# Raw weight blocks loaded ahead of the third and fourth attention chunk, and the first products moved accordingly

## The chip, the core and the metric

The kernel runs on one core of one Trainium2 chip. The metric is device time in microseconds of one execution. A profiled execution also gives a span, from its first to its last instruction.

## What is computed

Linear attention with decay over blocks of 64 positions, for 4 batches, 8 heads, 768 positions and a head size of 64; its output, as 3072 tokens of 512, goes through a two-layer network whose activation is h - tanh(h):

```
intra = einsum('bhic,bhjc->bhij', qb, kb) * Dmask[None]
intra = einsum('bhij,bhjd->bhid', intra, vb)
inter = einsum('bhid,bhde->bhie', qb * lam_pow[None], kv_state)
out[:, :, sl] = intra + inter
kv_state = lam_block * kv_state + einsum('bhsd,bhse->bhde', kb * rev_pow[None], vb)
...
h = x @ w_in            # 3072 x 512 by 512 x 2048
g = h - np.tanh(h)
return g @ w_out        # 2048 x 512
```

q, k, v are float32. The weights arrive as 64-bit floats, and the kernel reads them as pairs of 32-bit words.

## The kernel before

The sequence is cut into 6 groups of 128 positions; a group is taken for all 4 batches at once (512 tokens). One batch of a group is called a chunk here: chunks 0 to 3 are batches 0 to 3 of group 0. The change lies in group 0, the first some 40 us of the program.

**Loads.** All loads of this stage are issued by SP in the order of the program. `load(n)` issues q, k and v of chunks up to n (256 KB each, in pieces of 256 bytes). `load_weights(n)` issues raw blocks of `w_in` up to n: a block is 128 rows by 2 x 256 columns of 64-bit words, 512 KB. Blocks 0 and 1 of each unit come in one piece, blocks 2 and 3 in two halves of 64 rows. There are 16 blocks of `w_in`: block 4u + i holds rows i of unit u, and unit u is 512 of the 2048 hidden features. Four buffers hold raw blocks, so block n + 4 is loaded once block n is rounded as far as it reads the raw data.

**Rounding.** `round_block` makes a float32 block from a raw one. ScalarE makes two passes over it, called r (the low words, scaled, `AF.Copy`) and Abs (the high words, `AF.Abs`, into the block itself). VectorE then makes four passes: a clamp (L265), shift and mask (L267), the merge with the high word (L269) and the addition of r (L271). `weights(n)` rounds blocks up to n. For units 0 and 1 (`first`) the two ScalarE passes and the clamp are tied to the order of the program; the scheduler places the others.

**Attention.** For a chunk, `att_transpose` transposes q and k on TensorE (tp) and ScalarE copies them out (qt, kt); `att_decay` scales k by the decay on VectorE; `att_scores` forms the scores (sp), which VectorE multiplies by the mask (ss). For two chunks, `att_state` forms the state (kv), copied out by ScalarE, and `att_out` the output (op), which ScalarE copies to xt, the input of the first layer.

**First layer.** Group 0 goes through plain products. `up_plain(u, cs)` forms unit u for two of four quarters of its output, named 11, 21, 12 and 22: the second digit says which pair of chunks, the first which half of the unit's features. It is a generator: with `yield` between its steps the program puts other work between them. Each (i, c) is two products (h, 256 columns) by block i, so quarter 11 of unit u needs blocks 4u to 4u + 3 in turn. Then ScalarE forms the Tanh (th) and VectorE the difference (g).

In group 0 the work of TensorE, the copies of ScalarE and the masks of VectorE are tied: each engine has them in the order in which the program writes them. The second layer and the other five groups, which use two levels of Strassen-like products with weights from intermediate buffers in memory, are untouched.

Of the kernel before, what the change touches and what calls it, by code (L numbers as in the profile page):

```python
# [13 lines left out]
AF = mybir.ActivationFunctionType  # L14
# [9 lines left out]
def kernel(  # L24
# [32 lines left out]
    nc = tc.nc  # L57
    B, H, S, D = q.shape
# [3 lines left out]
    KI = DM // 128  # L62
# [55 lines left out]
    def tied(yes, op):  # L118
        return tc.keep_in_program_order(op) if yes else op
# [25 lines left out]
    def load(n):  # L145

        while at["loaded"] < min(n, len(chunks)):
            g, b = chunks[at["loaded"]]  # L150
            if g < GB:
                raw[g, b] = {}
                load_natural(g, b, "qkv")
                at["loaded"] += 1
                continue
            for b in range(B):
                raw[g, b] = {}
            nat = "kv" if g < NG - 1 else "v"

            first = (0, 1, 2) if g == GB else ()  # L160
            for b in first:
                load_natural(g, b, nat)
            for b in range(B - 1):
                load_blocks(g, b, "qk")
            load_blocks(g, 3, "q")
            for b in (0, 1):
                if b not in first:
                    load_natural(g, b, nat)
            load_blocks(g, 3, "k")
            for b in (2, 3):  # L170
                if b not in first:
                    load_natural(g, b, nat)
            at["loaded"] += B
# [31 lines left out]
    def load_weights(n):  # L205

        while ready["loaded"] < min(n, len(blocks)):
            if moe_w_in.dtype != F32:
                raw64 = stage.tile([128, 2, 256], I64, name="raw64", tag="raw64", bufs=WAHEAD)
                block = blocks[ready["loaded"]]  # L210
                load_block(nc.sync if block[0] == "in" else nc.gpsimd, raw64, *block, block[0] == "in")
                wraw[ready["loaded"]] = raw64
            ready["loaded"] += 1
# [38 lines left out]
    def round_block(w, raw64, first):  # L252


        word = raw64.rearrange("p a n -> p (a n)").bitcast(U32).rearrange("p (n w) -> p n w", w=2)
        wordf = raw64.rearrange("p a n -> p (a n)").bitcast(F32).rearrange("p (n w) -> p n w", w=2)
        lo, hi = word[:, :, 0], word[:, :, 1]
        w = w.rearrange("p a n -> p (a n)")
        wb, wi = w.bitcast(U32), w.bitcast(I32)

        r = stage.tile([128, 512], I32, name="r", tag="r", bufs=2)
        tied(first, nc.scalar.activation(r, lo, AF.Copy, scale=2.0 ** -29))  # L262

        tied(first, nc.scalar.activation(w, wordf[:, :, 1], AF.Abs))
        tied(first, nc.vector.tensor_scalar(out=w, in0=w, scalar1=CLAMP, scalar2=None, op0=AL.max))  # L265

        nc.vector.tensor_scalar(out=wb, in0=wb, scalar1=3, scalar2=0x3FFFFFF8, op0=AL.logical_shift_left,  # L267
                                op1=AL.bitwise_and)
        nc.vector.scalar_tensor_tensor(out=wb, in0=hi, scalar=0xC0000000, in1=wb, op0=AL.bitwise_and,  # L269
                                       op1=AL.bitwise_or)  # L270
        nc.vector.tensor_tensor(wi, wi, r, op=AL.add)  # L271

    def bank(name, tag, bufs):
        return psum.tile([128, 512], F32, name=name, tag=tag, bufs=bufs)


    load(B - 1)
    load_weights(2)
    load(B)
    load_weights(WAHEAD)  # L280

# [11 lines left out]
    def att_transpose(g, bs):  # L293
        for b in bs:
            load(g * B + b + 1)
            t = raw[g, b]
            qt = work.tile([128, NP, BLK], F32, name="qt", tag="qt")
            kt = work.tile([128, NP, BLK], F32, name="kt", tag="kt")
            for dst, x in ((qt, "q"), (kt, "k")):
                if g >= GB:  # L300
                    tc.keep_in_program_order(nc.vector.transpose(out=dst.rearrange("d p i -> d (p i)"),
                                                                 in_=t[x + "b"].rearrange("d p r a -> d (p r a)")))
                else:
                    tp = bank("tp", "att", 4).rearrange("d (p s) -> d p s", p=NP)
                    for p in range(NP):
                        tied(g == 0 or p == 0, nc.tensor.transpose(out=tp[:, p, :], in_=t[x][:, 2 * p:2 * p + 2, :],
                                                                   identity=ident))
                    tied(g == 0, nc.scalar.activation(dst, tp, AF.Copy))
            qd = None
            if g > 0:  # L310
                qd = work.tile([128, NP, BLK], F32, name="qd", tag="qd")
                nc.vector.tensor_tensor(qd, qt, fwd, op=AL.mult)
            tr[g, b] = (qt, kt, qd)

    def att_scores(g, bs):
        for b in bs:
            qt, kt, _ = tr[g, b]

            sp = [bank("sp", "att", 4).rearrange("s (p i) -> s p i", p=NP) for _ in range(2)]
            for p in range(NP):  # L320
                for j in range(2):
                    tied(g == 0, nc.tensor.matmul(out=sp[j][:, p, :], lhsT=kt[ts(j, 64), p, :],  # L322
                                                  rhs=qt[ts(j, 64), p, :], start=True, stop=True))
            ss = work.tile([128, 2, NP, BLK], F32, name="ss", tag="ss")
            for j in range(2):
                tied(g == 0, nc.vector.tensor_tensor(ss[:, j], sp[j], mask[:, j], op=AL.mult))  # L326
            sc[g, b] = ss

    def att_decay(g, b):
        kp = raw[g, b]["k"].rearrange("s (p j) d -> s p j d", j=2)  # L330
        tied(g != 1, nc.vector.tensor_tensor(kp, kp, bwd, op=AL.mult))

    def att_state(g, bs):
        if g == NG - 1:
            return

        kv = bank("kv", "att", 4).rearrange("d (b p e) -> d b p e", b=2, p=NP)
        for n, b in enumerate(bs):
            kd, vn = raw[g, b]["k"], raw[g, b]["v"]
            if g > 0:  # L340
                att_decay(g, b)
            for p in range(NP):
                for j in range(2):
                    tied(g == 0, nc.tensor.matmul(out=kv[ts(j, 64), n, p, :], lhsT=kd[:, 2 * p + j, :],  # L344
                                                  rhs=vn[:, 2 * p + j, :], start=n == 0 and p == 0, stop=True,
                                                  skip_group_check=True))
        st = state[:, bs[0]:bs[0] + 2]
        if g > 0:
            nc.vector.tensor_tensor(st, st, lam_blk, op=AL.mult)
            nc.vector.tensor_tensor(st, st, kv, op=AL.add)  # L350
        else:
            tied(True, nc.scalar.activation(st, kv, AF.Copy))
# [382 lines left out]
    def up_plain(u, cs):  # L735

        hm = {}
        for c in cs:
            a, t = divmod(c - 11, 10)
            hm[c] = bank("h", ("ya", "yb", "z", "w")[2 * t + a], 1).rearrange("q (m c) -> q m c", m=2)  # L740
        for i in range(KI):
            for c in cs:
                a, t = divmod(c - 11, 10)
                for m in range(2):
                    tied(u == 0, nc.tensor.matmul(  # L745
                        out=hm[c][:, m, :], lhsT=w1[u][:, i, a, ts(m, 128)], rhs=xt[0, t][:, i, :],
                        start=m == 0 and i == 0, stop=i == KI - 1, skip_group_check=True))
            if i + 1 < KI:
                yield
        for c in cs:  # L750
            th = work.tile([128, 2, HB], F32, name="th", tag="th")
            nc.scalar.activation(th, hm[c], AF.Tanh)
            nc.vector.tensor_tensor(hidden(0, c)[:, u], hm[c], th, op=AL.subtract)
        yield
# [24 lines left out]
    for b in (0, 1):  # L779
        att_transpose(0, (b,))  # L780
        att_decay(0, b)
        att_scores(0, (b,))
    att_state(0, (0, 1))
    att_transpose(0, (2,))
    att_decay(0, 2)
    weights(1)
    att_out(0, (0, 1))
    att_scores(0, (2,))
    half = up_plain(0, (11, 21))
    next(half)  # L790
    weights(2)
    att_transpose(0, (3,))
    att_decay(0, 3)
    att_scores(0, (3,))
    next(half)
    weights(KI)
    att_state(0, (2, 3))
    att_out(0, (2, 3))
    next(half)
    weights(KI + 2)  # L800
# [124 lines left out]
```

## Time and profile before

| | |
|---|---|
| time, median of 4 runs | 674.13 us (673.76 to 674.88) |
| the profiled execution's own time | 673.76 us |
| its span | 672.0 us |
| TensorE busy | 662.3 us (99%) |
| VectorE busy | 481.1 us (72%) |
| ScalarE busy | 194.8 us (29%) |
| GpSimd busy | 199.9 us (30%) |
| HBM read and written | 103.55 MB, 24.38 MB |

In the profile, PE is TensorE's products, PEld its weight loads, DVE is VectorE, ACT is ScalarE, POOL is GpSimd, and SP issues loads. A float32 product shows as two records. A row of the timeline has the start, the duration, the engine, the line, the operation and its tiles, and in brackets how long the engine had been idle and what ended that. A row of the waits has the waiting engine, what it wanted, who released it, the total, the number and the longest. "Landing" is the time from a load's issue to its last byte's arrival. In a row of windows each engine has its busy microseconds and, in brackets, its instructions.

### The profile page before, as it was taken

What the parts mean: (1) busy time and instruction counts of PE and PEld (TensorE: products, weight loads), DVE (VectorE), ACT (ScalarE), POOL (GpSimd) and SP (SyncE); (2) the same over time, 40 slices, a digit from 0 to 9 for tenths busy, and PEclk for the clock granted to TensorE, in tenths of its full rate; (3) what the DMA queues carried; (4) which work ended last, traced back from release to release, by engine and by line L of the source; (5) the groups of instructions that cost most, each with busy time, mean ns of one, the idle gap of its engine ahead of it and who ended that gap; (6) DMA issues with size and microseconds to landing.
All of it is one profiled execution on the core that took longest, in us unless ns stands there. A gap on an engine that the chain in (4) does not pass through costs nothing.

```text
span 672.0 us, 12866 instructions
## 1 busy us (share of the span) xinstructions
PE 662.3 (99%) x4824; PEld 577.4 (86%) x4824; DVE 481.1 (72%) x872; ACT 194.8 (29%) x373; POOL 199.9 (30%) x345
## 2 busy tenths in 40 slices
PE   8899999999999999999999999999999999999998
PEld 7688855558888999988999988899988899988897
DVE  4797857894887872399896378888358978357753
ACT  3664432423331111333112343112333112334110
POOL 0001424217332334144345200255300244400251
PEclk9899999999999999999999999999999999999999
DMA  9869788969955977487898741698840676610395
GB/s 207 218 192 246 250 250 253 309 145 258 259 142 131 242 202 211 112 256 216 224 297 248 199 85 43 152 288 236 254 81 4 156 247 199 227 49 1 109 299 171
DMA packets 162717, 128.80 MB, mean 192 GB/s; under 512 B 133856, under 2 KB 135008, under 8 KB 162656
## 3 DMA queue, kind: packets, MB, share of 16 engines
q0 software_dynamic: 28976, 96.49, 45.2%
q1 hardware_dynamic: 133536, 31.50, 23.6%
q8 instruction: 38, 0.62, 0.4%
q14 instruction: 23, 0.19, 0.1%
q10 hardware_dynamic: 144, 0.00, 0.0%
HBM read 103.55 MB, written 24.38 MB: 190 GB/s over the span
## 4 chain that ended last, share of the span: by engine, by line
PE 97%; DMA 2%; SPq 1%; DVE 0%; ACT 0%; issue 0%; ACTq 0%
PE y L428 17%; PE y L690 11%; PE z L428 10%; PE zw L690 8%; PE h L745 8%; PE op L766 8%; PE w L637 5%; PE y L637 5%; PE y L512 4%; PE plain L637 3%; PE sp L322 3%; PE op L376 3%; PE z L512 2%; PE op L370 2%; PE kv L344 1%; PE w L512 1%
## 5 line engine op out<-in xcount | busy, mean ns | idle before, releaser
L602 POOL DMA_DIRECT2D wb<-fine x147 | 79.2, 539 | 113.7 <-PE y L690 48.6
L436 ACT ACTIVATE th<-g 128x512 f32<-128x512 f32 x76 | 47.6, 630 | 98.9 <-DVE g L441 33.2
L605 POOL DMA_DIRECT2D wb<-factors x56 | 30.2, 541 | 153.7 <-PE y L637 97.3
L428 PE MATMUL y<-xt,w 128*128 128x256 f32 x320 | 74.0, 380 | 0.0
L428 PEld LDWEIGHTS y<-xt,w 128*128 128x128 f32 x320 | 59.9, 190 | 9.0 <-ACT g L516 0.9
L437 DVE TENSOR_TENSOR g<-g,th 128x512 f32<-128x512 f32 x76 | 51.9, 688 | 18.5 <-ACT th L436 18.4
L693 ACT ACTIVATE q<-y 128x128 f32<-128x128 f32 x84 | 23.3, 277 | 129.0 <-PE y L690 125.4
L745 PE MATMUL h<-xt,w 128*128 128x256 f32 x256 | 56.7, 383 | 2.2 <-DVE w L271 2.2
L745 PEld LDWEIGHTS h<-xt,w 128*128 128x128 f32 x256 | 48.6, 191 | 9.2 <-ACT r L262 2.3
L766 PE MATMUL op<-wt,g 128*128 128x512 f32 x128 | 56.5, 595 | 0.0
L690 PE MATMUL y<-wb,g 128*128 128x128 f32 x384 | 51.1, 278 | 0.0
L766 PEld LDWEIGHTS op<-wt,g 128*128 128x128 f32 x128 | 23.8, 190 | 27.7 <-issue 26.5
L690 PEld LDWEIGHTS y<-wb,g 128*128 128x128 f32 x384 | 46.4, 192 | 1.1 <-issue 0.3
L428 PE MATMUL z<-tt,ws 128*128 128x256 f32 x160 | 38.0, 380 | 0.0
L428 PE MATMUL z<-xt,ws 128*128 128x256 f32 x160 | 37.9, 380 | 0.0
L428 PE MATMUL y<-tt,ws 128*128 128x256 f32 x160 | 37.8, 379 | 0.0
L198 POOL DMA_DIRECT2D raw<-in_moe_w_out_dram x16 | 8.8, 553 | 91.7 <-DMA raw<-in_moe_w_in_dram 53.2
L637 PE MATMUL y<-wb,g 128*128 128x256 f32 x160 | 35.6, 379 | 0.5 <-PE y L428 0.5
L637 PE MATMUL w<-wb,g 128*128 128x256 f32 x160 | 35.8, 382 | 0.0
L326 DVE TENSOR_TENSOR ss<-sp,mask 128x512 f32<-128x512 f32 x48 | 31.0, 683 | 6.2 <-PE sp L322 6.2
L637 PEld LDWEIGHTS y<-wb,g 128*128 128x128 f32 x160 | 30.3, 190 | 5.0 <-PE y L428 0.9
L428 PEld LDWEIGHTS z<-xt,ws 128*128 128x128 f32 x160 | 30.3, 190 | 4.3 <-ACT g L444 0.2
(171 smaller groups left out, 1302.3 us busy)
## 6 DMA issues: line engine op xcount, KB each, us to landing
wb<-fine POOLq DMA_DIRECT2D x147, 256.0 KB, 3.9
wb<-factors POOLq DMA_DIRECT2D x68, 256.0 KB, 4.2
raw<-in_moe_w_out_dram POOLq DMA_DIRECT2D x16, 512.0 KB, 5.3
v_nat<-in_v_dram SPq DMA_DIRECT2D x24, 256.0 KB, 5.3
factors<-wt POOLq DMA_DIRECT2D x8, 768.0 KB, 4.7
wb<-fine_in POOLq DMA_DIRECT2D x24, 256.0 KB, 4.1
k_nat<-in_k_dram SPq DMA_DIRECT2D x20, 256.0 KB, 5.0
raw<-in_moe_w_in_dram SPq DMA_DIRECT2D x8, 512.0 KB, 6.0
```

The source lines that it names most:

```text
L326: tied(g == 0, nc.vector.tensor_tensor(ss[:, j], sp[j], mask[:, j], op=AL.mult))
L428: nc.tensor.matmul(out=t[:, m, :], lhsT=wt[:, kt, ts(m, 128)], rhs=x[:, kt, :], start=first and m == 0 and kt == 0, stop=kt == 1, skip_gro ...
L436: nc.scalar.activation(th, src, AF.Tanh)
L437: nc.vector.tensor_tensor(dst(c), src, th, op=AL.subtract)
L512: nc.tensor.matmul(out=dst[:, ts(u, 128)], lhsT=a, rhs=b, start=x in (1, 2, 5) and u == 0, stop=True, skip_group_check=True)
L602: nc.gpsimd.dma_start(out=t.rearrange("p m c -> p (m c)"), in_=fine[TWICE.index(n_), SUB.index(x_)].rearrange("p u c -> p (u c)"))
L605: nc.gpsimd.dma_start(out=t, in_=factors[XAT[FACT[n_][1]]][:, 2 * x_:2 * x_ + 2, :])
L637: nc.tensor.matmul(out=t[:, m, :], lhsT=a[:, u, kt, ts(m, 128)], rhs=wb[:, kt, :], start=first and u == 0 and m == 0 and kt == 0, stop=u = ...
L690: nc.tensor.matmul(out=dst, lhsT=a[:, u, :], rhs=wb[:, ts(u, 128)], start=x in (1, 2) and u == 0, stop=u == NU - 1, skip_group_check=True)
L693: nc.scalar.activation(keep, dst, AF.Copy)
L745: tied(u == 0, nc.tensor.matmul(out=hm[c][:, m, :], lhsT=w1[u][:, i, a, ts(m, 128)], rhs=xt[0, t][:, i, :], start=m == 0 and i == 0, stop= ...
L766: nc.tensor.matmul(out=obank[b], lhsT=g, rhs=wt[:, 2 * a:2 * a + 2, :], start=kt == 0 and a == 0, stop=kt == KH - 1 and a == 1)
```

## The change

SP's first loads go from q, k, v of chunks 0, 1 and 2, raw blocks 0 and 1, chunk 3, raw blocks 2 and 3, to: chunks 0 and 1, raw blocks 0 and 1, chunk 2, raw block 2, chunk 3, raw block 3.

On TensorE, the output of chunks 0 and 1 comes ahead of the transposes of chunk 2, unit 0's first four products (block 0) ahead of the scores of chunk 2, two products with block 1 ahead of the transposes of chunk 3 and two behind them, and the four products with block 2 between the state and the output of chunks 2 and 3. To allow this, `up_plain` yields after each (i, c) but the last, not after each i. Rounding moves along: block 0 after the scores of chunk 1, block 1 after the state of chunks 0 and 1, block 2 after the scores of chunk 2, blocks 3 and 4 after the state of chunks 2 and 3. In `round_block` the Abs pass comes before the r pass.

```diff
+        tied(first, nc.scalar.activation(w, wordf[:, :, 1], AF.Abs))
+
         r = stage.tile([128, 512], I32, name="r", tag="r", bufs=2)
         tied(first, nc.scalar.activation(r, lo, AF.Copy, scale=2.0 ** -29))
-
-        tied(first, nc.scalar.activation(w, wordf[:, :, 1], AF.Abs))
         tied(first, nc.vector.tensor_scalar(out=w, in0=w, scalar1=CLAMP, scalar2=None, op0=AL.max))
...
-    load(B - 1)
+    load(2)
     load_weights(2)
+    load(3)
+    load_weights(3)
     load(B)
     load_weights(WAHEAD)
...
-            if i + 1 < KI:
-                yield
+                if (i, c) != (KI - 1, cs[-1]):
+                    yield
...
         att_scores(0, (b,))
+    weights(1)
     att_state(0, (0, 1))
+    weights(2)
+    att_out(0, (0, 1))
+    half = up_plain(0, (11, 21))
     att_transpose(0, (2,))
     att_decay(0, 2)
-    weights(1)
-    att_out(0, (0, 1))
+    next(half)
+    next(half)
     att_scores(0, (2,))
-    half = up_plain(0, (11, 21))
+    weights(3)
     next(half)
-    weights(2)
     att_transpose(0, (3,))
     att_decay(0, 3)
+    next(half)
     att_scores(0, (3,))
+    att_state(0, (2, 3))
     next(half)
-    weights(KI)
-    att_state(0, (2, 3))
+    next(half)
+    weights(KI + 1)
     att_out(0, (2, 3))
     next(half)
     weights(KI + 2)
```

## The prediction

> **What bounds the kernel now.** First the page: who is busy, and at what clock. Then the waits of the whole span, for TensorE alone.
>
> ```profile
> PE 662.3 (99%) x4824; PEld 577.4 (86%) x4824; DVE 481.1 (72%) x872; ACT 194.8 (29%) x373; POOL 199.9 (30%) x345
> PE h L745 <- DVE w L271: 2.2, 1, 2.2
> PE sp L322 <- ACT kt L308: 2.1, 3, 0.7
> ```
>
> TensorE is the bound; behind the start its waits come to 0.5 us. All that a reordering can win lies in the first 31 us: two idle times are large enough to count, and one is unit 0's first product waiting for rounded block 0. The timeline of the first 25 us shows how it comes about:
>
> ```profile
> 10.55 1.99 SPq L200 DMA_DIRECT2D raw<-in_moe_w_in_dram  x2
> 14.08 4.43 SPq L130 DMA_DIRECT2D v_nat<-in_v_dram  x1
> 15.87 0.68 ACT L262 ACTIVATE r<-raw 128x512 int32<-128x512 uint32 x1 [0.67 <-DMA raw<-in_moe_w_in_dram]
> 19.63 2.61 PE L745 MATMUL h<-xt,w 128*128 128x256 f32 x8 [2.18 <-DVE w L271]
> 22.88 1.06 PE L306 MATMUL tp<-ident,k_nat 128*128 128x128 f32 x4
> 24.69 1.16 PE L322 MATMUL sp<-qt,kt 64*128 64x128 f32 x16 [0.75 <-ACT kt L308]
> ```
>
> Raw block 0 is behind nine q/k/v tiles in SP's queue and lands at 15.85; rounding ends at 19.48, and TensorE has been out of work since 17.44. The windows by microsecond show a second price: the columns behind the engines are granted clock, DMA share, GB/s.
>
> ```profile
> 18.00:19.00 1.00, 0.00 (x0) 0.00 (x0) 0.93 (x3) 0.31 (x2) 0.00 (x0) 1.00 0.65 128
> 21.00:22.00 1.00, 1.00 (x3) 0.65 (x3) 0.93 (x3) 0.00 (x0) 0.00 (x0) 0.50 1.00 195
> ```
>
> The clock is at half from 20.9 to 24.3 us. Eight h records take 2.61 us there against 1.99 later, two transposes 2.12 against 1.25: 1.5 us.
>
> From 30.53 TensorE never stops, but VectorE is almost as full (4.93 of 5 us in 35 to 40), because it rounds unit 1's blocks:
>
> ```profile
> 37.52 0.68 DVE L271 CUSTOM_DVE_ANT_0 w<-w,r 128x1024 uint16<-128x1024 uint16 x1
> 41.85 0.68 DVE L753 TENSOR_TENSOR g<-h,th 128x512 f32<-128x512 f32 x1
> 42.45 0.68 DVE L271 CUSTOM_DVE_ANT_0 w<-w,r 128x1024 uint16<-128x1024 uint16 x1
> ```
>
> The last line finishes block 7 at 43.13. The chain of waits has 136 h records in 29.55 us from 30.60, 217 ns each; the 61st, unit 1's first with block 7, is due at 30.60 + 60 x 0.217 = 43.6. So only 0.5 us of slack is left here. Behind it there is much: block 11 is ready at 52.9 for a product due at 57.5, block 15 at 67.5 for one past 71. What the change is worth is therefore TensorE's start on block 7, against 43.6.
>
> **The change part by part.**
>
> *Loads.* Bytes are the same. Landing times (issue plus time to landing) are 10.9 for v of chunk 1, 12.1, 13.3, 14.4 for chunk 2, 15.85 and 18.7 for raw 0 and 1, 19.4, 20.5, 22.6 for chunk 3. A q/k/v tile costs 1.15 us of the stream, a raw block in one piece 1.45, a raw half about 1.1 (23.6, 24.7). Blocks 0 and 1 now follow 10.9 directly: block 0 lands at 12.4. Behind it the old sequence (raw, raw, q, k, v, raw 2) repeats 3.5 us earlier: raw 1 at 15.3, q, k, v of chunk 2 at 16.0, 17.0, 19.1, raw 2 at 21.2. Then q and k of chunk 3 at 22.4 and 23.5. That is the late end. In that old sequence raw 1 came 1.4 late, v's issue took 4.43 us, and traffic fell to 128 GB/s in 18 to 19. Without that loss k of chunk 3 lands at 10.9 + 2.9 + 3.45 + 2.2 + 2.3 = 21.8, the early end. I take 22.6, about the middle: the copied row has the lag, but the two halves of raw 2 now stand where the queue can work some of it off.
>
> *Rounding.* The Abs pass before the r pass starts VectorE 0.6 us sooner per tied block. Block 0: 12.4 + 0.66, VectorE free at 13.7 after ss of chunk 1, four passes 2.3: ready at 16.0, not 19.48. Block 1: 15.3 + 0.66 + 2.3 = 18.3. On ScalarE, xt of the first half is now queued behind block 1's two passes (to 16.6), then qt and kt of chunk 2: kt ends at 18.9 and nobody lacks it, as sp of chunk 2 comes after four h products, at 19.5 (without them it would be 1 us of idle time).
>
> *Costed at nothing.* SP: raw 4 and later loads stay in their order and wait for buffers that come free sooner (block 0's third pass at 15.2, not 18.7). GpSimd: one load of output weights changes places with a store of factors at about 72 us, 10 us before TensorE takes the first of all output weights (82.4). The products' order within unit 0 only changes which of two banks is filled first. If the GpSimd cover failed, it would cost one landing, 5.3 us by its row, less that slack.
>
> *TensorE's walk.* kv and op of chunks 0, 1 end at 15.3 to 15.6; q waits to 16.0, k to 17.0 (0.9 us idle in all); h with block 0 at 17.6 once xt is there, not at 19.63; sp 19.5; h with block 1 at 20.6 to 21.5. Then it waits for chunk 3: q at 21.5, k at 22.6, h to 24.1, sp to 25.2, kv to 26.3. The two removed idle times (2.18 and 0.75) thus come back as waits for chunk 2 and 3, about 1.9 us in all; the order itself is better, because four more h products lie before kv. If block 7 did not matter, TensorE would be at it at about 41.5: 2.1 us gained.
>
> *What is late next: block 7.* ScalarE takes block 3 after the state copy that follows kv: Abs at 27.0, VectorE starts at 27.6. From there to the end of block 7 the old trace needs 29.33 to 43.13, 13.8 us with 0.8 us idle; the new order has the same passes and one more (block 8's third, 0.6, ahead of block 7's last): 27.6 + 13.6 = 41.2 if nothing waits. But two waits are put into the queues. On VectorE block 8's first pass stands before block 6's last. On ScalarE block 9's Abs stands before both Tanh passes of unit 0's second half, and the product g behind the first Tanh stands before block 7's last pass. Block 9's load is issued once block 5's third pass ends, 27.6 + 4.6 + 2.0 = 34.2. Its row before took 5.0 us (37.33 to 42.3), block 8's 3.9 (34.14 to 38.05): landing 38.1 to 39.2. Then Abs, r, Tanh, g, last pass: 0.6 x 4 + 0.7 = 3.1 gives 41.2 to 42.3, and queueing behind block 8 adds up to 0.3. I take 42.1.
>
> *Sum.* 43.6 - 42.1 = 1.5 us. The profiled execution took 673.76 (span 672.0 and 1.76 around it): 672.26. It is the fastest of the four runs; the median lies 0.37 above: 672.6. The half clock is not a term of its own: removing it brings TensorE to block 7 sooner, where it waits.
>
> On the clock the row is an idle time of 2.18 us, followed by 3.41 us at half speed, while 0.69 us of idle time had none; the new waits (1.1 and less in one place) lie between the two, so I count none as the likeliest and price one below. The Trainium skill, TensorE: Matmul & The Clock Gate, HAM oscillation, says that the clock falls at idle gaps longer than about 3.4 us; by it the new waits could never do it, but nor could the 2.18, so the trace decides here. By the page the sum would be the same 672.6 and the slow case below would go.
>
> **The rivals.**
>
> *More comes through.* Chunk 3 lands near the early end and block 9 takes 3.9 us: block 7 at 40.5 to 41.5, gain 2.1 to 3.1, 670.7 to 672.0. For it: the stream's own rates. Against it: raw 1 was late by 1.4, and block 9, the same rows of the weights for unit 2, was also slower than block 8.
>
> *Given back at block 7.* The late end, k at 23.5: everything behind sp shifts by 0.9, block 7 at 43.0 to 43.6, gain 0 to 0.6: 673.5 to 674.1. For it: the sequence of transfers is literally the old one. That the change moves nothing is excluded; the built order differs in all five queues.
>
> *Slower: chunk 3 behind three weight blocks starves TensorE until the clock halves.* It decides from k landing at about 24.3: then TensorE idles some 2.2 us between 21.5 and 24.3, as much as in the row that cost a half clock. For it: raw 2 is put ahead of chunk 3, and every lag of raw 1 is inherited. Against it: k would have to come 0.8 later than the copied sequence says, and the wait is split by q's transposes. Sp and kv come 1.7 to 2.0 later than in the forecast, and a half clock of 3.41 us costs 1.1 to 1.7 more; block 7 at 44.9 to 45.8, a loss of 1.3 to 2.2, 675.4 to 676.3.
>
> **How the numbers follow.** Forecast, gain 1.0 to 2.0 (672.1 to 673.1): 0.42. More: 0.22. Given back: 0.18. Slower: 0.18. The range 671.0 to 675.7 leaves out a third of "more" (0.07) and two thirds of "slower" (0.12). 0.2% is 1.35 us, about what a measurement of this kernel can tell from no change. Of the forecast 0.26 lies beyond it, with "more" 0.48 faster; 0.16 and 0.18 make 0.34 the same; 0.18 slower. As cases of both signs hold much of the chance: the forecast's own range is 672.1 to 673.1.
>
> **What would show it.** Right: h's first record near 17.6, no wait of h for L271 of 2 us there; transposes of chunk 3 waiting for q_nat and k_nat, k's about 22.7; a new wait of h for L271 near 41.5 to 42.1; ScalarE waiting for a raw landing before the Tanh at about 40. Wrong: k later than 23.5, a clock of 0.5 after 21 us, or no wait at block 7 at all (then the gain is TensorE's walk, and my VectorE chain was too long).

## The result, and the profile after

The changed kernel takes 675.92 us in the median of 37 runs (673.03 to 679.67), the kernel before 674.33 in 58 runs (672.02 to 675.55) beside it. The ratio is 1.0027, with a 95% interval from 1.0020 to 1.0034: slower by 0.27%, which is 1.8 us (the medians lie 1.6 apart), where 672.6 was predicted and the range ended at 675.7. The profiled execution of the changed kernel took 674.21 us (span 672.4), 0.45 more than that of before, and 1.7 less than the changed kernel's own median. So two things need a cause: why the predicted 1.5 us did not come, which this first profile shows, and why a usual run is worse than this profile, for which a second one is needed. "Raw 5" is short for the load of raw block 5.

The page and the waits of TensorE, after:

```profile
PE 661.1 (98%) x4824; PEld 575.1 (86%) x4824; DVE 481.5 (72%) x872; ACT 194.7 (29%) x373; POOL 199.9 (30%) x345
```

```profile
PE tp L308 <- DMA q_nat<-in_q_dram: 1.6, 1, 1.6
PE tp L308 <- DMA k_nat<-in_k_dram: 1.5, 3, 0.6
PE h L747 <- DVE w L271: 1.1, 1, 1.1
```

TensorE is still the bound, and 1.2 us less busy (before: 662.3); the granted clock is 1.00, with no stretch at half. The wait of 2.18 us for block 0 is gone. In its place stand waits for chunk 3's q and k, and a new one for a rounded block, 1.1 us long. The timeline of after tells which block:

```profile
16.82 1.89 PE L747 MATMUL h<-xt,w 128*128 128x256 f32 x8
22.50 0.63 PE L308 MATMUL tp<-ident,q_nat 128*128 128x128 f32 x4 [1.64 <-DMA q_nat<-in_q_dram]
23.51 0.63 PE L308 MATMUL tp<-ident,k_nat 128*128 128x128 f32 x4 [0.37 <-DMA k_nat<-in_k_dram]
30.93 11.73 PE L747 MATMUL h<-xt,w 128*128 128x256 f32 x52
31.12 0.67 ACT L261 ACTIVATE w<-raw 128x512 f32<-128x512 f32 x1 [2.14 <-DMA raw<-in_moe_w_in_dram]
36.63 0.55 SPq L200 DMA_DIRECT2D raw<-in_moe_w_in_dram  x1
40.68 0.69 ACT L261 ACTIVATE w<-raw 128x512 f32<-128x512 f32 x1 [1.53 <-DMA raw<-in_moe_w_in_dram]
41.84 1.07 ACT L754 ACTIVATE th<-h 128x512 f32<-128x512 f32 x2
42.46 0.69 DVE L755 TENSOR_TENSOR g<-h,th 128x512 f32<-128x512 f32 x1
43.07 0.68 DVE L271 CUSTOM_DVE_ANT_0 w<-w,r 128x1024 uint16<-128x1024 uint16 x1
43.80 2.43 PE L747 MATMUL h<-xt,w 128*128 128x256 f32 x10 [1.15 <-DVE w L271]
```

Block 0's products start 2.8 us sooner than before (19.63). TensorE has done all that lies ahead of block 7 at 42.66, about 1 us sooner than before; then it waits, and starts on block 7 at 43.80, which before was due at 43.6. Block 7's last add (43.07) is behind the product g (42.46), that behind a Tanh (41.84), and that on ScalarE behind the Abs of block 9 (40.68), which had waited for its raw data. The chain of waits adds a second path to the same add:

```profile
23.61 9.87 DMA raw<-in_moe_w_in_dram
33.49 0.68 ACT w L261
...
35.89 0.68 DVE w L269
...
41.16 1.29 DVE w L269 x2
42.46 0.69 DVE g L755
43.15 0.61 DVE w L271
43.80 16.24 PE h L747 x74
```

Raw 5 took 9.87 us and landed at 33.47 (29.82 before). Block 5's third pass (35.89) ended at 36.57, which freed the buffer for raw 9, issued at 36.63 (above). From 35.9 VectorE worked without a pause until g, with block 8's third pass (one of the two L269) among block 7's. In this execution VectorE and the Tanh came free within 0.1 us of each other.

How raw 5 came to be late begins with the stream and with SP's queue. The window of after in which v of chunk 3 blocks SP's queue (issued at 17.32, in 3.91 us):

```profile
21.00:22.00 1.00, 0.00 (x0) 0.00 (x0) 0.12 (x1) 0.14 (x1) 0.00 (x0) 1.00 0.20 35
```

The traffic falls to 35 GB/s. Before, the gap in 18 to 19 was 128 GB/s. The row in which SP issues raw 4 and 5, before and then after:

```profile
21.39 1.43 SPq L200 DMA_DIRECT2D raw<-in_moe_w_in_dram  x2
```

```profile
22.94 1.22 SPq L200 DMA_DIRECT2D raw<-in_moe_w_in_dram  x2
```

Raw 3 still lands as before (27.41 and 27.43), but raw 4 and 5 land at 31.10 and 33.47 instead of 28.54 and 29.82. A part of this is the issue: in SP's queue they stand behind v of chunk 3 and raw 3, and so are issued 1.55 and 1.35 us later than before. The rest is a longer transfer: 8.2 and 9.9 us from issue to landing, instead of 7.2 and 7.6.

### The profile page after: what moved, and what is told of

Read it like the earlier page. It is cut to its first block, busy times and chain, and to the rows that moved or that the text cites. A ratio compares the mean times of both kernels' runs of the same rounds, so it can differ in the third digit from the quotient of the medians.

```text
span 672.4 us, 12865 instructions
## 1 busy us (share of the span) xinstructions
PE 661.1 (98%) x4824; PEld 575.1 (86%) x4824; DVE 481.5 (72%) x872; ACT 194.7 (29%) x373; POOL 199.9 (30%) x345
## 4 chain that ended last, share of the span: by engine, by line
PE 94%; DMA 3%; DVE 1%; SPq 1%; ACT 0%; issue 0%
PE y L430 16%; PE y L692 11%; PE z L430 10%; PE zw L692 8%; PE op L768 8%; PE h L747 6%; PE w L639 5%; PE y L639 5%; PE y L514 4%; PE plain L639 3%; PE sp L324 3%; PE op L378 3%; PE z L514 2%; PE op L372 2%; DMA raw<-in_moe_w_in_dram 1%; PE kv L346 1%
## 5 line engine op out<-in xcount | busy, mean ns | idle before, releaser
L768 PEld LDWEIGHTS op<-wt,g 128*128 128x128 f32 x128 | 23.8, 190 | 27.7 <-issue 26.5
```

Source lines behind the costliest of these rows:

```text
L768: nc.tensor.matmul(out=obank[b], lhsT=g, rhs=wt[:, 2 * a:2 * a + 2, :], start=kt == 0 and a == 0, stop=kt == KH - 1 and a == 1)
```

## The experiments

Ratios are to the kernel before, run beside each; a ratio is not the quotient of the two medians, and lies up to 0.1% from it, once 0.26%. "Late blocks" is the theory that block 7 sets the loss, behind raw loads and the order on ScalarE; "starved TensorE" the one that the waits for chunk 3 and the clock set it.

**The changed kernel again.** No edit.

> The changed kernel once more, for its time beside the others and for a second profile. 'Late blocks' (raw 4 and raw 5 land 2.5 to 3.6 us later than before, block 9's Abs stands ahead of unit 0's last Tanh, block 7 is ready at 43.75): block 7 ends the wait again, at 43.5 to 45, and a run that is 1 to 2 us longer has this wait longer. 'Starved TensorE' (waits for chunk 3 halve the clock in some runs): a run with clock 1.00 stays near the 674.2 of the first profile, a run with 0.997 or less is 1.0 to 1.5 longer, and the median of about 675.9 is a mixture. Both: 675 to 676.5, 1.0 to 2.0 above the kernel before.

675.25 us beside 674.23; 1.0005, 0.9991 to 1.0019. Weaker than in the first comparison, and alone not told from no change. The profiled run took 675.66, with the clock at 1.00 throughout. Its timeline:

```profile
35.59 0.55 SPq L200 DMA_DIRECT2D raw<-in_moe_w_in_dram  x1
42.10 0.69 ACT L261 ACTIVATE w<-raw 128x512 f32<-128x512 f32 x1 [2.52 <-DMA raw<-in_moe_w_in_dram]
43.24 1.05 ACT L754 ACTIVATE th<-h 128x512 f32<-128x512 f32 x2
43.84 0.69 DVE L755 TENSOR_TENSOR g<-h,th 128x512 f32<-128x512 f32 x1 [0.99 <-ACT th L754]
45.19 1.13 PE L747 MATMUL h<-xt,w 128*128 128x256 f32 x4 [2.48 <-DVE w L271]
```

Raw 9 was issued 1 us sooner than in the first profile and landed 1.4 later. Here VectorE is idle ahead of g, so raw 9 alone sets the wait: 2.48 us, 1.33 more than the first profile's, in an execution that is 1.45 longer. That is most of the difference between the two, with no part for the clock, which is 1.00 in both. In both, block 7 is ready 3.1 us after raw 9's landing (43.75 and 45.13).

**Tanh ahead of block 9's Abs.**

```diff
-                round_block(w, wraw.pop(at_), at_ < 2 * KI)
+                round_block(w, wraw.pop(at_), at_ < 2 * KI + 2)
...
-            nc.scalar.activation(th, hm[c], AF.Tanh)
+            tied(u == 0, nc.scalar.activation(th, hm[c], AF.Tanh))
```

> The changed kernel with the order of ScalarE and VectorE written out for two more blocks: unit 0's last two Tanh stand ahead of the Abs of blocks 8 and 9, so that block 7's last add no longer waits behind raw 9's landing (40.66 in the changed kernel). 'Late blocks': block 7 is ready at 40.5 to 42.5 rather than 43.75, TensorE goes on at 42.66 without its wait of 1.15 us, 1.0 to 1.2 us faster than the changed kernel (674.5 to 675.2), if block 11 is not late in its turn. 'Starved TensorE': no difference beyond 0.3 us, since chunk 3's waits at 20 to 24 us are as they were. 'Order of the passes itself costs': no difference or slower.

673.82 us, 1.43 below the changed kernel on the same chip; 0.9992 (0.9978 to 1.0007) to before. This interval overlaps that of the run above (0.9991 to 1.0019), but not that of the first comparison (1.0020 to 1.0034). The timeline:

```profile
31.15 15.16 PE L747 MATMUL h<-xt,w 128*128 128x256 f32 x69
40.14 0.60 ACT L754 ACTIVATE th<-h 128x512 f32<-128x512 f32 x1 [0.27 <-PE h L747]
41.04 0.68 DVE L271 CUSTOM_DVE_ANT_0 w<-w,r 128x1024 uint16<-128x1024 uint16 x1
```

Block 7 is ready at 41.7, two microseconds sooner, and TensorE goes through without a wait. The waits for chunk 3 were as before the edit (1.69 and 0.48 us). The edit takes block 8's passes out of block 7's way as well, so it does not part the two paths of the chain above; as TensorE's earlier waits stayed, it does show that the loss lies at block 7.

**r ahead of Abs, one part of the change undone.**

```diff
-        tied(first, nc.scalar.activation(w, wordf[:, :, 1], AF.Abs))
-
         r = stage.tile([128, 512], I32, name="r", tag="r", bufs=2)
         tied(first, nc.scalar.activation(r, lo, AF.Copy, scale=2.0 ** -29))
+
+        tied(first, nc.scalar.activation(w, wordf[:, :, 1], AF.Abs))
```

> The changed kernel with one part undone: the low-word pass r stands ahead of Abs in each block again. With it the planner puts unit 0's two last Tanh around block 9's Abs, the first of them ahead of it, as in the kernel before; in the changed kernel both stood behind it. 'Late blocks' (block 7's last add stands behind those Tanh and so behind raw 9's landing): TensorE's wait at block 7 of 1.15 and 2.48 us in the two profiles of the changed kernel falls under 0.4, although each block's first pass comes 0.6 later; time 0.8 to 1.5 below the changed kernel, 673.6 to 674.8. 'Order of the passes is worth what it was written for' (0.6 us for block 0): time the same as the changed kernel or up to 0.6 longer. 'Starved TensorE': no difference beyond 0.3, waits for chunk 3 as they were.

674.72 us beside 674.25; 1.0010 (0.9994 to 1.0026), in time not told from the changed kernel or from before. What it shows lies in its profile. There the wait at block 7 is gone too, by another edit; raw 9 landed at 42.57, later than in either profile of the changed kernel, and it did no harm, because the first Tanh stood ahead of its Abs:

```profile
31.82 50.34 PE L747 MATMUL h<-xt,w 128*128 128x256 f32 x232 [0.81 <-DVE w L271]
39.90 0.59 ACT L754 ACTIVATE th<-h 128x512 f32<-128x512 f32 x1
42.59 0.68 ACT L264 ACTIVATE w<-raw 128x512 f32<-128x512 f32 x1 [2.10 <-DMA raw<-in_moe_w_in_dram]
```

A wait of 0.81 us for block 3 came instead, since each block's first pass is later. So this order on ScalarE was made by two parts of the change together: with Abs first and the new order of products, the scheduler put two Abs (blocks 8 and 9) in a row ahead of unit 0's Tanh.

**Raw 6 held back.**

```diff
+                if ready["loaded"] == 6:
+                    tied(True, nc.vector.memset(raw64.rearrange("p a n -> p (a n)").bitcast(F32)[:, 0:1], 0.0))
```

> The changed kernel; the load of raw 6 is held back by a write of one column of its buffer after chunk 3's masked products, so that it is issued at about 27.5 rather than 24.3, as before (28.8). 'Late blocks', with raw 6's bytes as the cause: raw 4 lands at 29 to 30 and raw 5 at 30.5 to 32 rather than 31.10 and 33.47, ScalarE's waits of 2.14 and 0.17 us shrink by 1 to 2 us, and block 7 is ready 0 to 0.9 us sooner (not the whole, since raw 9 still stands ahead of Tanh): 0 to 0.9 us faster than the changed kernel. With the blocked v issue of chunk 3 as the cause alone: raw 4 and raw 5 land within 0.5 us of where they did, and the time stays. 'Starved TensorE': time stays within 0.3 us.

674.76 us; 1.0001 (0.9988 to 1.0014), 0.5 below the changed kernel, within what was left open. Raw 4 and 5 landed at 29.49 and 31.81, but without the hold the second profile of the changed kernel has 29.00 and 31.98. So nothing here shows that raw 6 makes raw 5 late; of what I suspected, the blocked v issue is left, and it is not shown. A wait of 0.99 us at block 7 stayed.

**The fourth chunk ahead of raw 2 again.**

```diff
-    load(3)
-    load_weights(3)
     load(B)
```

> The changed kernel with one part of it undone: the fourth chunk's q, k and v are loaded ahead of raw 2 again (two raw blocks stay ahead of the third chunk). 'Starved TensorE': q3 and k3 land some 2 us sooner (20.3 and 21.3), the waits of 1.64 and 0.37 us shrink to under 0.3, the clock is 1.00 in nearly all runs and the time 1 to 2 us below the changed kernel. 'Late blocks': raw 2 lands at 23.5 to 25 as before the change, so the h products of block 2 come a little later; raw 4 and raw 5 land 0 to 1 us sooner as v3's issue comes earlier; block 7 still behind raw 9: time within 0.7 us of the changed kernel.

679.33 us; 1.0050 (1.0033 to 1.0066). Both theories missed this. q and k of chunk 3 land at 19.19 and 20.31, but raw 2 at 24.93, and block 2's Abs is tied ahead of chunk 3's k copy on ScalarE. The timeline:

```profile
21.63 1.03 PE L745 MATMUL h<-xt,w 128*128 128x256 f32 x4
26.55 0.60 ACT L308 ACTIVATE kt<-tp 128x512 f32<-128x512 f32 x1
27.20 2.08 PE L322 MATMUL sp<-qt,kt 64*128 64x128 f32 x16 [4.54 <-ACT kt L308]
```

TensorE idles 4.54 us and then works at half clock (2.08 us for scores that take 1.16). The rounding's place on ScalarE and the load's place on SP must move together: this is the same fault as at block 9, on a larger scale.

**Chunk 3 first, with other products to fill.** On top of Tanh first:

```diff
     load(3)
+    raw[chunks[3]] = {}
+    load_natural(*chunks[3], "qk")
     load_weights(3)
-    load(B)
+    load_natural(*chunks[3], "v")
+    at["loaded"] += 1
...
     att_scores(0, (2,))
-    weights(3)
     next(half)
...
     att_scores(0, (3,))
+    weights(3)
     att_state(0, (2, 3))
+    att_out(0, (2, 3))
     next(half)
     next(half)
-    weights(KI + 1)
-    att_out(0, (2, 3))
-    next(half)
     weights(KI + 2)
-    every(half)
+    other = up_plain(0, (12, 22))
+    for _ in range(2 * (KI - 1)):
+        next(other)
     weights(2 * KI)
-    every(up_plain(0, (12, 22)))
+    every(half)
+    every(other)
```

> A version made from what the first four runs show: Tanh first as in the second of them; q and k of chunk 3 are loaded ahead of raw 2, v behind it; block 2 is rounded behind chunk 3's k copy; chunk 3's output products stand ahead of block 2's products, and unit 0's second half (blocks 0 to 2) ahead of block 3 of the first. 'Starved TensorE' and 'late blocks' together: q3 and k3 land at 20.3 and 21.4, the waits of 1.69 and 0.48 us fall under 0.5 in sum, TensorE reaches block 7 at about 41.5 instead of 42.8 and block 7 is ready at 40.8 to 41.8: span 670 to 670.7, time 0.8 to 1.5 below the one with Tanh first alone, 672.3 to 673.2 in the median. If TensorE's wait for chunk 3 is not what counts, or block 7 comes no sooner than 42.5: within 0.4 of the one with Tanh first alone. If block 2 is late in its turn (over 28.5): slower by 0.5 to 1.5.

673.63 us; 0.9996 (0.9983 to 1.0010): no different from Tanh first alone. The waits for q and k of chunk 3 fell to 0.23 us, but TensorE then waited 1.26 us for v of chunk 3, and at 40.23 another 1.21 us for a g pass that had to empty a bank: the Tanh of the first half had been pushed back with its last block.

**The loads alone, and Abs first alone.** The two edits of the diff, each in the kernel before.

> The kernel before with the new load order alone (raw 0 and raw 1 ahead of chunk 2, raw 2 ahead of chunk 3), compute and rounding as before. TensorE has chunk 2's transposes queued ahead of the first chunks' output products, so these wait for k2 (16.2): output products at 16.8 rather than 14.4, first products of block 0 at 20.5 to 21.5 rather than 19.63, score products of chunk 3 at 24.8 to 25.5 rather than 24.69. 'Late blocks': Tanh stay ahead of block 9's Abs, block 7 is ready within 0.7 of 43.1, and the time is 0 to 1 above the kernel before. 'Loads cost by themselves through late raw 4 and raw 5': 1 to 2 above the kernel before, with a wait at block 7 of over 0.5. 'Starved TensorE': a longer half-clock stretch, 0.5 to 1.5 above.

> The kernel before with the order of two ScalarE passes alone changed, Abs ahead of r in each block. On ScalarE the Tanh stay ahead of block 9's Abs here. 'Late blocks': block 0 is ready 0.57 sooner, TensorE's wait of 2.18 falls to 1.6, block 7 is ready 0 to 0.6 sooner and no wait appears there: 0 to 0.6 below the kernel before. 'Abs first costs by itself': 0.5 to 1.5 above the kernel before, with a wait at block 7.

The loads alone: 675.95 us; 1.0029 (1.0017 to 1.0041), a wait of 2.12 us for chunk 2's q and 1.38 us for block 0, none at block 7. So the new loads in the old order of products are as slow as the whole change (1.0027), but by other waits: raw 9 landed at 43.42, later than in any profile of the changed kernel, and held nothing up, as the first Tanh (41.81) stood ahead of its Abs.

Abs alone: 672.95; 0.9986 (0.9974 to 0.9998). Here the scheduler left the first Tanh (40.50) ahead of block 9's Abs (41.29). The profile, of the longest of its 12 runs (674.78), has no shorter wait for block 0, which was the point of the edit: raw 0 landed at 16.27 (15.85 before), and half clock followed.

```profile
19.59 3.06 PE L745 MATMUL h<-xt,w 128*128 128x256 f32 x8 [2.14 <-DVE w L271]
```

**v of chunks 2 and 3 behind k of chunk 3**, which takes them out of the way of all that is needed sooner; three times: in the changed kernel, with Tanh first, and with Abs alone (there raw 0 and 1 follow k of chunk 2).

```diff
-    load(3)
+    raw[chunks[2]], raw[chunks[3]] = {}, {}
+    load_natural(*chunks[2], "qk")
     load_weights(3)
-    load(B)
+    load_natural(*chunks[3], "qk")
+    load_natural(*chunks[2], "v")
+    load_natural(*chunks[3], "v")
+    at["loaded"] = B
```

> The changed kernel with its loads alone in another order: v of chunks 2 and 3 behind k of chunk 3 (v is not read before the state products at 26). q3 and k3 land at about 19.8 and 21 instead of 22.4 and 23.4, raw 2 at 19.5, raw 3 and all behind it as they were; the order on the compute engines is the same. 'Late blocks': TensorE's waits of 1.64 and 0.37 us for chunk 3 fall under 0.5 in sum, TensorE reaches block 7 about 1 us sooner, and there it waits as much longer (2.2 to 3.5 us) for block 7, which is ready when raw 9 lets it: time within 0.5 of the changed kernel, apart from fewer runs with a half-clock stretch (up to 0.6 less in the median): 674.6 to 675.8. 'Starved TensorE': what is gained at chunk 3 stays: 1 to 2 below the changed kernel, 673.3 to 674.7.

> The same load order together with Tanh first. 'Late blocks': block 7 is ready at about 41.7 as with Tanh first alone, TensorE reaches it at 41.3 to 42 instead of 42.8, so that now the time saved at chunk 3 comes through: 0.6 to 1.2 below Tanh first alone (673.82), 672.4 to 673.3; with the run before this one it is the test, since the same edit should be worth next to nothing there and about 1 us here. 'Starved TensorE': worth the same 1 to 2 in both. Rival: v3 is late for the state products by over 1 us and takes the gain back: 673.5 to 674.

> The kernel before with Abs ahead of r and with v of chunks 2 and 3 loaded behind k of chunk 3: raw 0 lands near 14.7 instead of 15.85 to 16.3, block 0 is ready at about 17.4, TensorE's wait of 2.1 us ahead of its products falls under 0.6, clock 1.00 in nearly all runs. Block 7 stays at 42.6 to 43.1, since its rounding goes on as before; TensorE is there at 41 to 41.7 and waits 1 to 2 us. 'Late blocks': about 0.3 to 0.8 below Abs first alone (672.95) or the same, 672.2 to 673.0, and no more, although 2 us are freed at the start. 'Starved TensorE': 1.5 to 2 below Abs first alone.

The kernel before took 674.07 beside them. Changed kernel: 674.33, 1.0012 (0.9994 to 1.0030). Tanh first: 673.12, 0.9987 (0.9978 to 0.9995). Abs alone: 672.44, 0.9978 (0.9969 to 0.9986).

As a test of the two theories it failed. By the medians the edit moved the changed kernel by some 0.8 us against before and the one with Tanh first by 0.5, where I had expected nothing and 1; by the ratios (1.0005 to 1.0012, and 0.9992 to 0.9987), whose intervals overlap, neither move is shown. The profile of the changed kernel with this edit says why it could not be a test: with the stream in this order raw 9 was issued at 35.06, and landed at 39.05:

```profile
39.07 0.69 ACT L261 ACTIVATE w<-raw 128x512 f32<-128x512 f32 x1 [1.52 <-DMA raw<-in_moe_w_in_dram]
40.24 1.07 ACT L758 ACTIVATE th<-h 128x512 f32<-128x512 f32 x2
41.46 0.68 DVE L271 CUSTOM_DVE_ANT_0 w<-w,r 128x1024 uint16<-128x1024 uint16 x1
```

Same order on every compute engine as in the changed kernel, and no wait of TensorE at block 7. Three profiles of one order now read: raw 9 at 39.05, no wait; 40.66, 1.15 us; 42.08, 2.48 us. In all three block 7 is ready 3.05 to 3.10 us after that landing. Raw 4 and 5 landed at 29.05 and 31.51 here, though v's issues were shorter (2.17 and 1.22 us) and stood elsewhere; that is about where they landed in the second profile of the changed kernel, which speaks against the blocked v issue as the cause. And in both kernels TensorE, freed at chunk 3, met block 3 too early (waits of 0.70 and 1.14 us), which hangs on raw 3.

The last of the three, Abs alone with v late, is the best of the versions tried, 1.6 us faster than before in one comparison of 11 runs. Where the kernel before idles 2.18 us, its timeline has 0.96, at full clock:

```profile
18.43 1.97 PE L750 MATMUL h<-xt,w 128*128 128x256 f32 x8 [0.96 <-DVE w L271]
23.16 1.99 PE L750 MATMUL h<-xt,w 128*128 128x256 f32 x8
30.48 13.86 PE L750 MATMUL h<-xt,w 128*128 128x256 f32 x63 [0.58 <-DVE w L271]
```

It gained what was expected, but by luck: the wait of 1 to 2 us at block 7 that I had put there did not come. And it loads nothing ahead of the third chunk's q and k.

**The idle stretch of before, filled.**

```diff
     att_scores(0, (2,))
+    for _ in range(10):
+        tied(True, nc.tensor.matmul(out=idle[:, 0:128], lhsT=ident, rhs=ident, start=True, stop=True))
     half = up_plain(0, (11, 21))
```

> The kernel before with ten products of the identity on TensorE, into a bank that is not in use, ahead of the first products of block 0, where it waits 2.18 us; nothing else is moved. If that wait is what halves the clock for some 3.4 us afterwards (two thirds of the runs of the kernel before have a granted clock of 0.997, and these are 1.5 to 1.9 longer than those with 1.00): clock 1.00 in nearly all runs, and the median near that of the kernel before's runs at 1.00, 672.9 to 673.5, 0.8 to 1.4 below its median. If the half clock comes from elsewhere: same as before within 0.3. If the ten products are in the way: 0.2 to 0.5 longer.

674.85 us beside 674.07; 1.0010 (0.9998 to 1.0021). The mechanism was right: 10 of 12 runs had a granted clock of 1.00 and 2 of 0.999, against 10 and 6 of 35 of the kernel before, and eight h records took 1.89 us instead of 2.61:

```profile
19.71 1.89 PE L745 MATMUL h<-xt,w 128*128 128x256 f32 x8
```

The price was not: nothing was gained. The first profile, the shortest run, has TensorE at the second layer at 81.30 instead of 82.44, so the time is freed there; that other runs lose it later was the next guess.

**Raw 9 held back**, by the same write as for raw 6, on its buffer, in the changed kernel and with Tanh first; and the filled kernel again.

```diff
+                if ready["loaded"] == 9:
+                    tied(True, nc.vector.memset(raw64.rearrange("p a n -> p (a n)").bitcast(F32)[:, 0:1], 0.0))
```

> The changed kernel; the load of raw 9 is held until block 5's last add by a write of one column of its buffer, so that it is issued at about 37.9 rather than 36.6; the order of all other work is as in the changed kernel. 'Late blocks' with raw 9's landing as the thing that sets the wait: TensorE's wait at block 7 grows by the delay, and the time by 0.8 to 1.5 over the changed kernel, 676.2 to 677.2 (1.8 to 3.0 above the kernel before of these runs). 'Starved TensorE', or a loss elsewhere: no difference beyond 0.4, 675 to 676.

> The same hold of raw 9 in the kernel with Tanh first. 'Late blocks': nothing of unit 0 stands behind raw 9 there, block 7 is ready at about 41.7 as before, and blocks 8 to 11 have slack: within 0.4 of Tanh first alone (0.4 below the kernel before, as measured beside it). If a late raw 9 costs by itself (blocks 9 to 11): 0.5 to 1.3 longer than that, as in the run before this one.

> The kernel before with the ten products once more, for a second profile: its first, at 673.26, was the shortest of its 12 runs (median 674.85), with the clock at 1.00. 'Late blocks': a run of typical length has a wait of 1 to 2 us ahead of an h product of units 0 to 3, behind a rounded block or a g pass that stands behind a load (raw 8 to raw 11 landing 1 to 2 us later than in the first profile). 'Loss elsewhere': no such wait before 82 us, TensorE reaches the first output product at 81.3 as in the first profile, and the difference lies in the last 40 us or ahead of the first product.

675.22, 675.10 and 674.65 us beside 674.49; 1.0017 (1.0004 to 1.0029), 1.0010 (0.9999 to 1.0021) and 1.0009 (0.9993 to 1.0024). The first missed its expectation (676.2 to 677.2) and is no test of it: with the write in it the scheduler put the first Tanh (40.60) ahead of block 9's Abs (42.25), which I had taken to stay as it was. It shows something else. TensorE waits at block 7 all the same:

```profile
43.38 39.12 PE L749 MATMUL h<-xt,w 128*128 128x256 f32 x180 [0.95 <-DVE w L273]
```

The chain of waits of this profile goes back from block 7 through VectorE, where block 8's passes stand among those of blocks 6 and 7, and through ScalarE's passes of blocks 7 and 8, to the landing of raw 7 at 36.99, and not to raw 9. So late loads of unit 1 can hold block 7 up by the second path alone.

The second missed its expectation too: 0.6 above before instead of 0.4 below. With Tanh first block 10's Abs stands ahead of those of blocks 8 and 9; in the profile it waits 3.58 us for its load, until 45.96, and the second layer waits 0.70 us for a g pass at 85.67. So holding raw 9 back, and raw 10 with it, was not free in that order; how much of the 0.6 is this wait, the runs do not show. The third, a run of 675.53, shows a g wait of 0.68 us at 75.26 and, new, waits of 0.89 and 0.93 us at 304.96 and 313.03 for `wb<-factors`, weight blocks of a later group.

**Before, Abs alone and filled, side by side.** No new edits.

> The kernel before as it is, for a second profile beside the two below. If waits for factor blocks at 304 and 312 us (0.89 and 0.93 us in the second look at the filled kernel) come in runs of every kernel: a run at or above its median shows them here too, or a late g pass at 75 us. If they come only where TensorE is there sooner: none here, and the only idle time is that of the start (2.18 and 0.75 us) and the 0.54 us at 304.

> Abs ahead of r alone, again. If the shorter wait ahead of block 0 (1.6 instead of 2.18 us) keeps the clock and this is worth the 1.3 us that the first run showed: 672.7 to 673.4, clock 1.00 in two thirds of the runs or more, and a profile with clock 1.00 reaches the first output product at 81 to 81.6 us. If the first run was chance: within 0.4 of the kernel before.

> The ten products once more, beside the two above on the same chip. If a kept clock is worth about 1.3 us: below the kernel before by 0.8 or more, as Abs alone. If what is kept at the start is lost again at later waits for loads: within 0.8 of the kernel before on either side, clock 1.00 in nearly all runs, and the profile shows waits after 82 us that add up to 0.7 or more.

673.66, 673.41 and 674.45 us beside 674.14: 0.9996 (0.9984 to 1.0008), 0.9995 (0.9985 to 1.0005), 1.0012 (1.0002 to 1.0022). Abs alone is not told from before this time, so its gain of 1.3 us is not established. Its timeline, of an execution of 674.38 us:

```profile
19.09 1.96 PE L745 MATMUL h<-xt,w 128*128 128x256 f32 x8 [1.65 <-DVE w L271]
80.56 7.03 PE L766 MATMUL op<-wt,g 128*128 128x512 f32 x16
302.91 0.67 PE L637 MATMUL y<-wb,g 128*128 128x256 f32 x2 [0.84 <-DMA wb<-factors]
310.80 3.72 PE L637 MATMUL y<-wb,g 128*128 128x256 f32 x16 [0.75 <-DMA wb<-factors]
650.18 1.13 PE L690 MATMUL zw<-wb,g 128*128 128x128 f32 x8 [0.45 <-DMA wb<-fine]
```

The wait for block 0 is the 1.6 us that was expected, the clock is kept, and the second layer starts at 80.56, 1.9 us sooner than before. Then all of it goes: 0.84 and 0.75 us for factor blocks, 0.45 and more near the end. In the filled kernel:

```profile
304.59 0.67 PE L637 MATMUL y<-wb,g 128*128 128x256 f32 x2 [1.38 <-DMA wb<-factors]
645.06 1.13 PE L690 MATMUL zw<-wb,gS 128*128 128x128 f32 x8 [1.12 <-DMA wb<-fine]
```

Neither profile of the kernel before has such a wait, though the second is of a run above its median; their second layers start at 82.44 and 82.61. What sets the blocks at 304 is GpSimd's queue, where a load of factors stands behind the landing of a write-back. In the kernel before:

```profile
297.22 0.76 POOL L596 DMA_DIRECT2D wb<-factors  x1 [2.25 <-DMA fine<-wb]
298.50 0.55 POOL L605 DMA_DIRECT2D wb<-factors  x1
```

The second load lands at 303.09, and TensorE reads it at 304.47: 1.4 us of slack. In the filled kernel the queue waited 4.42 us for the write-back, issued that load at 299.95, and TensorE waited for it.

## Why the prediction was wrong

The step that failed is the landing of raw 9, taken at 38.1 to 39.2 and measured at 40.66 and 42.08; under it lies a term put at nothing, the loads from raw 4 on. The steps, in the prediction's order.

*Loads: right up to chunk 3, and not worked out behind it.* Raw 0 landed at 12.39 (12.4 predicted), raw 2 at 21.77 (21.2), q of chunk 3 at 22.37 (22.4). k landed at 23.37, the late end, not at the 22.6 I took. Raw 4 and 5 were "costed at nothing", with the reason that their buffers come free sooner. The buffers did, but they were not what these loads waited for: already before, raw 4 was issued at 21.39, with its buffer free at 18.7. It waited for its turn in SP's queue, and that came 1.55 us later. Raw 4 and 5 landed 2.6 and 3.7 us later in the first profile, 0.5 and 2.2 in the second.

*TensorE's walk: sound, 1 us late.* It ended at 42.66, not 41.5; 0.8 of it is k. The predicted waits for q and k are there, 1.64 and 0.37.

*Block 7: the mechanism was right, the term failed.* The prediction names the path that the profile shows, block 9's Abs ahead of both Tanh, g ahead of block 7's last pass. Its 42.1 rests on a landing of raw 9 between 38.1 and 39.2, and that on block 5's third pass ending at 34.2. With raw 4 and raw 5 late, that pass ended at 36.57 and the load was issued at 36.63. It then took 4.03 us in one profile and, issued at 35.59, 6.49 in the other, against a predicted 3.9 to 5.0. Block 7 was ready at 43.75 in the first, 1.65 later than taken, and about 1.4 later still in the second. This is the step that failed: one landing, 1.5 to 4 us too early in the sum, on a path that I had found and then sized with block 5's pass on time. The 3.1 us from landing to ready was right. In the three profiles of this order the values of the landing make the difference between no wait and 2.48 us. The second path, VectorE's own queue behind the late loads of unit 1, was in the prediction as "41.2 if nothing waits"; in the profile with raw 9 held it ended at 43.32.

*Sum.* TensorE starts on block 7 at 43.80, 0.2 us later than the 43.6 of before instead of 1.5 sooner, and the profiled execution took 674.21, 0.45 more. For the median I added 0.37, from the runs of before. The changed kernel's first profile lies 1.7 below its median, and its runs spread more (673.03 to 679.67, against 672.02 to 675.55), so that offset could not be carried over. The second profile, near the median, has the later landing; for the other runs, which have no profile, this cause is argued and not shown.

*The slack behind block 7.* "Behind it there is much" was true of blocks 11 and 15, not of the program: the load at 304 has 1.4 us. Even a start 1.5 to 2 us sooner would have been kept in full only in some runs.

*The clock.* No half clock was counted, and the profile has none. Over the runs it is a matter of degree: in the first comparison 18 runs of the changed kernel had 1.00 and 17 had 0.997; of the kernel before, beside the experiments, 46 and 93. The loss is there at either clock: these means are 675.36 against 673.46 us at 1.00, and 676.52 against 674.67 at 0.997, and side by side in the second comparison 674.77 (4 runs) against 673.43 (11), and 675.91 (6) against 674.91 (20). So the clock does not make it. The Trainium skill, TensorE: Matmul & The Clock Gate, HAM oscillation, puts the fall at idle gaps of more than about 3.4 us. The wait of 4.54 us, with half clock behind it, agrees. The shorter ones do not: 2.18 us in the kernel before was followed by half clock, 1.65 us in Abs alone was not; in the profile of Tanh first with raw 9 held, waits of 1.66 and 0.38 us within three microseconds were followed by half clock from 23.8 to 27, while 1.64 and 0.37 in the changed kernel's were not.

*The rivals.* "Given back at block 7", at 673.5 to 674.1, comes close to the first profile, k at 23.4 and block 7 at 43.75. The median lies where "Slower" put it, 675.4 to 676.3, but not for its reason: chunk 3's waits are the same in the kernel with Tanh first, which is 1.4 us faster. None of the prediction's three signs of being wrong came: k landed before 23.5, the clock stayed at 1.00 in the profile, and there was a wait at block 7. No sign was set on the loads behind chunk 3.

Left open: why the transfer of raw 5 takes longer in the profiles of the new load order (it landed at 31.0 to 33.5), and whether an earlier start makes the later waits at 304 and 645 more likely or only lays them bare. Waits of TensorE for `wb` loads of 0.3 us or more stand in six of the nine profiles that reach the second layer before 82 us, and in four of the eleven others; that is too few to decide.

## What to carry to other kernels

An engine that works strictly in order passes the lateness of any load in its queue to all that stands behind it; when a change lets a scheduler reorder, read the built order for passes that wait for a transfer and stand ahead of work on the bound path, and price them with the worst landing in the trace, and with the issue that the queue in front of it allows, not with the moment its buffer is free. Move a load and the pass that reads it together, and first move out of the way what is read last (here v), before loading anything ahead of what is read next. A gain at the start can be lost at a later stage, so look for loads there that land just before their use. It need not be: Abs alone with v late came to the read at 304 1.8 us sooner than before (302.69) and did not wait for its factors, because its load was issued sooner too and landed at 300.63.

## What the runs showed of the hardware that was not expected

The same load of 512 KB, raw 9, took from 3.99 to 6.49 us from issue to landing in three profiles with the same order of work on the compute engines. Runs of the kernel before with a granted clock of 0.997 are 1.2 us longer in the mean than those with 1.00 (674.67 in 93 runs, 673.46 in 46), and yet ten products of the identity, which kept the clock at 0.999 or 1.00 in 27 of 32 runs, gained nothing in three comparisons. At the same clock of 1.00 the filled kernel took 674.59 us in the mean of 22 runs, 1.1 more than the kernel before in its 46. So the difference between the two sorts of runs is not what a kept clock is worth, or the filled kernel loses as much elsewhere; the waits at 304 and 645 are the candidates, and the products themselves are not excluded.
